# A four-layer attention kernel: its plan counts TensorE's semaphore records, and its order tables are replaced

## The chip, the cores and the metric

The kernel runs on one core of a Trainium2 chip. A core has a matrix engine (TensorE, PE in the profile; its weight loads are the rows PEld), a vector engine (VectorE, DVE), an activation engine (ScalarE, ACT), a general engine (GpSimd, POOL) and a queue engine that here only issues DMAs (SyncE, SP). Each engine works through its own instructions in order and waits on semaphores for the others. The metric is the device time of one execution in microseconds (us). Less is better.

## The reference

A stream `x` of 2048 tokens by 512 goes through four layers, A, B, A, B, each with a layer norm ahead of it and added back to the stream. Both kinds of layer have 32 heads of 16. In an A layer a token attends to 8 tokens at distances 0, 2, ..., 14 behind it; in a B layer to the 256 tokens up to itself.

```
x = A_x
x = x + A(layernorm(x), A_wqkv, A_wo)      # idx = pos - 2*arange(8), mask idx >= 0
x = x + B(layernorm(x), B_wqkv, B_wo)      # mask 0 <= q - k < 256
x = x + A(layernorm(x), A_wqkv, A_wo)
x = x + B(layernorm(x), B_wqkv, B_wo)
# in each: qkv = x @ wqkv; softmax(q k^T / 4 over the kept keys) v; concatenate heads; @ wo
```

## The kernel before

**Tiling.** The stream is cut into 8 chunks of 256 tokens. Chunk `c` of layers 0 and 1 is written by the scopes A0..A7 and B0..B7, that of layers 2 and 3 by A8..A15 and B8..B15; the scopes S, pA, pB hold constants and weights, W holds 122 TensorE tasks that compute nothing that is used (L1761). Large products are made in float16 halves: each projection part multiplies a high and a low half (L1032 to L1034 and L1052 to L1055). A layer A makes scores with small matmuls of 32 rows (L1191, 64 in one task), brings them into bands through DRAM, and mixes values with L1300 (64 in one task). A layer B stacks q and k through DRAM (puts of `re` at L1342, then `stack`), makes scores twice, once for the row maximum (L1418, reduced by VectorE at L1433) and once transposed (L1569, exponentials on ScalarE at L1579 and L1591), masks the triangles on GpSimd (L1608) or VectorE (L1602), and multiplies by the values (L1624).

**The plan.** Nothing of this is issued where it is written. Each step is a `Task` with an engine, a time, the values that it reads and writes, and buffers. `Plan.order` runs a small model of the core over all 7702 tasks and issues them in the order in which the model starts them. Within one engine the order is not the model's choice: each task has a place, a number from the table `ORDER` (one list for each scope, one number for each task), and each engine's queue is sorted by it (line 563). A negative number stands for the task's other engine: a mask on VectorE in place of GpSimd, a put on ScalarE's queue in place of SP's, and so on (line 524). So the table holds the whole order of each of the five engines and the choices between two engines, and it was found by a search that is not in the file. The model's times decide how the five queues are interleaved in the program and which PSUM bank and which buffer a task gets.

**What the model knows of instructions.** It counts TensorE's instructions as `n`, from 3, and `t.rec` for each task: 6 by default (three matmuls and three weight loads), 64 for a task of L1624, 128 for one of L1191, 129 for one of L1300. By that count it places three events in each packet of 256 instructions, and makes the task wait that reaches the third too early (lines 643 to 650; `SUPPLY` is 5.0):

```
for x in range(n + 1, n + t.rec + 1):
    if x % 256 == 152:
        mark = now + wait + us * (x - n) / t.rec
    elif x % 256 == 168:
        asked, told = told, max(mark, now, told + SUPPLY if told else 0.0)
    elif x % 256 == 193 and x > 256:
        wait = max(wait, asked + SUPPLY - now - us * (x - n) / t.rec)
n += t.rec
```

[...]

Of the kernel before, what the change touches and what calls it, by code (L numbers as in the profile page):

```python
# [19 lines left out]
S = 2048  # L20
# [5 lines left out]
W = 8  # L26
# [652 lines left out]
def kernel(  # L679
# [1084 lines left out]
    for l in (0, 2):  # L1764
        for c in range(NCH):
            n = (l // 2) * NCH + c
            plan.begin(f"A{n}")
            layer_a(l, c)
            plan.begin(f"B{n}")
            layer_b(l + 1, c)  # L1770
# [30 lines left out]
```

## Time and profile before

| | us |
|---|---|
| median of 3 runs | 1445.88 |
| lowest and highest run | 1444.29, 1458.36 |
| the profiled execution | 1450.96 |
| its span, from the first to the last instruction | 1449.2 |
| TensorE busy | 1319.0 (91%) |
| VectorE busy | 863.3 (60%) |
| ScalarE busy | 824.9 (57%) |
| GpSimd busy | 380.6 (26%) |

The mean granted TensorE clock is 0.967 of full speed. A row of the groups names the line, the engine, the operation, the tiles, the count, then the busy time, the mean of one in ns, and the idle time of that engine just before, with what ended it. A row of the waits names who waited, for whom, the sum in us, how many times, and the longest. A row of the busy times by stretches has the stretch, its length, for each engine the busy time and (x) the number of its instructions that lie in or reach into the stretch, then the granted clock, the DMA engines' busy share, and GB/s.

### The profile page before, as it was taken

The numbers are of one execution on the slowest core, as the hardware profiler recorded it, in microseconds if no ns is written. First come the engines' busy times: TensorE is split into PE (matmuls) and PEld (weight loads), VectorE is DVE, ScalarE is ACT, GpSimd is POOL, SyncE is SP. The second block draws the span as 40 slices with busy tenths as digits, with TensorE's granted clock in tenths as the row PEclk, the third lists the DMA queues.
The fourth block names the chain that finished last, engine by engine and source line by source line (L and its number), as shares of the span: only waits on it lengthen the run. The fifth ranks groups of instructions, "written<-read, shape, count | busy, mean of one in ns | idle before, by whom it ended". The sixth has DMA issues, their size and how long they took to land.

```text
span 1449.2 us, 62327 instructions
## 1 busy us (share of the span) xinstructions
PE 1319.0 (91%) x27206; PEld 844.3 (58%) x27206; DVE 863.3 (60%) x1945; ACT 824.9 (57%) x1304; POOL 380.6 (26%) x800
## 2 busy tenths in 40 slices
PE   8999999998998989889899898888989899988988
PEld 7766456574565746547465554645656465564645
DVE  6546664746657474465755536465573755728485
ACT  7654557464665736547474554737657365653554
POOL 5411122222432232112250121423132222331231
PEclk9999999999999999999999998999999999999999
DMA  9865445636364462554527464363544626445241
GB/s 297 206 179 156 111 113 140 159 97 172 99 169 113 137 164 58 160 126 137 130 76 180 122 167 119 93 169 92 170 122 137 166 75 155 105 139 134 71 113 55
DMA packets 203659, 195.08 MB, mean 135 GB/s; under 512 B 92893, under 2 KB 147933, under 8 KB 203385
## 3 DMA queue, kind: packets, MB, share of 16 engines
q1 hardware_dynamic: 177264, 172.63, 43.9%
q10 hardware_dynamic: 26120, 18.46, 5.1%
q8 instruction: 213, 3.49, 1.1%
q14 instruction: 62, 0.50, 0.1%
HBM read 94.11 MB, written 79.36 MB: 120 GB/s over the span
## 4 chain that ended last, share of the span: by engine, by line
PE 59%; DMA 10%; ACT 7%; DVE 6%; issue 6%; SPq 4%; ACTq 2%; POOL 0%; DVEq 0%; POOLq 0%
PE banks L1624 7%; PE banks L1032 7%; PE banks L1033 6%; PE banks L1034 6%; PE banks L1054 6%; PE banks L1052 5%; PE banks L1055 5%; PE banks L1418 5%; PE banks L1569 5%; PE banks L1300 3%; DVE m L1433 2%; PE banks L1191 2%; ACT p L1579 2%; DMA ptt<-ptd 1%; SPq L1342 1%
## 5 line engine op out<-in xcount | busy, mean ns | idle before, releaser
L1433 DVE TENSOR_REDUCE m<-banks 128x2 f32<-128x512 f32 x448 | 302.4, 688 | 9.0
L1579 ACT ACTIVATE p<-banks,sclB 128x896 f32<-128x896 f32 x224 | 221.1, 1008 | 87.9 <-PE banks L1569 68.2
L1437 DVE COPY_PREDICATED banks<-trm,banks 128x128 f32<-128x128 int16 x448 | 124.5, 291 | 158.1 <-PE banks L1418 131.2
L1608 POOL TENSOR_SCALAR_AFFINE_SELECT p<-p 64x256 f32<-64x256 f32 x272 | 106.7, 414 | 353.5 <-ACT p L1579 318.3
L1418 PE MATMUL banks<-stk_k,stk_q 48*64 48x320 f16 (+4 forms) x2560 | 139.6, 273 | 27.5 <-DVE m L1433 7.7
L1569 PE MATMUL banks<-stk_q,stk_k 64*64 64x256 f16 (+3 forms) x3584 | 121.4, 242 | 29.6 <-DVE m L1433 5.4
L1608 POOL TENSOR_SCALAR_AFFINE_SELECT ps<-ps 64x256 f32<-64x256 f32 x264 | 104.0, 416 | 163.3 <-ACT ps L1591 158.8
L1624 PE MATMUL banks<-p,v 64*32 64x192 f32 (+1 forms) x3584 | 119.5, 364 | 17.8 <-issue 15.0
L1418 PEld LDWEIGHTS <-stk_q 48*64 48x64 f16 x2560 | 64.1, 107 | 118.9 <-issue 103.2
L1591 ACT ACTIVATE ps<-banks,sclB 128x768 f32<-128x768 f32 x112 | 100.3, 901 | 44.0 <-PE banks L1569 32.0
L1569 PEld LDWEIGHTS <-stk_k 64*64 64x64 f16 x3584 | 71.6, 109 | 90.0 <-issue 73.5
L1200 ACT COPY s<-banks 128x624 f32<-128x624 f32 x64 | 74.7, 1260 | 44.2 <-PE banks L1191 33.0
L1638 DVE TENSOR_TENSOR os<-os,banks 128x256 f32<-128x256 f32 x112 | 46.3, 417 | 82.2 <-ACT os L1641 78.0
L1624 PEld LDWEIGHTS banks<-p,v 64*32 64x32 f32 x3584 | 63.7, 108 | 48.0 <-issue 26.2
L1641 ACT COPY os<-banks 128x256 f32<-128x256 f32 x112 | 41.4, 372 | 86.9 <-PE banks L1624 67.6
L1332 DVE SCALAR_TENSOR_TENSOR el<-banks,eh 128x512 f16<-128x512 f32 x64 | 42.6, 687 | 80.7 <-ACT eh L1329 69.2
L1624 PE MATMUL banks<-ps,v 64*32 64x64 f32 (+1 forms) x3584 | 70.0, 250 | 10.5 <-issue 10.4
L1624 PEld LDWEIGHTS banks<-ps,v 64*32 64x32 f32 x3584 | 63.7, 107 | 19.0 <-issue 16.8
L1032 PE MATMUL banks<-xh,wA1h 128*128 128x256 f16 x256 | 72.2, 282 | 1.5 <-ACT v L1367 1.5
L1032 PE MATMUL banks<-xh,wA0h 128*128 128x256 f16 x256 | 71.9, 281 | 0.9 <-issue 0.6
L1034 PE MATMUL banks<-xh,wA0l 128*128 128x256 f16 x256 | 71.3, 278 | 0.8 <-issue 0.8
L1033 PE MATMUL banks<-xl,wA1h 128*128 128x256 f16 x256 | 71.5, 279 | 0.0
(202 smaller groups left out, 3080.7 us busy)
## 6 DMA issues: line engine op xcount, KB each, us to landing
sd<-s SPq DMA_DIRECT2D x100, 156.0 KB
ptt<-ptd SPq DMA_DIRECT2D x128, 96.0 KB
stk_k<-re SPq DMA_DIRECT2D x128, 96.0 KB
stk_q<-re SPq DMA_DIRECT2D x128, 96.0 KB
re<-eh SPq DMA_DIRECT2D x82, 128.0 KB
vs<-vd SPq DMA_DIRECT2D x64, 156.0 KB
vd<-ve SPq DMA_DIRECT2D x32, 256.0 KB
xm<-y SPq DMA_DIRECT2D x32, 256.0 KB
```

What stands on the lines that cost most here:

```text
L1032: nc.tensor.matmul(ps[mp].t[:, i], wh, xh, start=k == 0, stop=False)
L1033: nc.tensor.matmul(ps[mp].t[:, i], wh, xl, start=False, stop=False)
L1034: nc.tensor.matmul(ps[mp].t[:, i], wl, xh, start=False, stop=k == 3)
L1054: nc.tensor.matmul(ps.t, xh.t[:, k, tk], wh, start=k == 0, stop=False)
L1418: nc.tensor.matmul(o, lhs, k, start=True, stop=True, tile_position=(64 * par, 64 * h))
L1433: nc.vector.tensor_reduce(out=m.t[:, :, u, qb], in_=ps.t[:, :, 0 : 2 * P], op=ALU.max, axis=AX.X)
L1437: nc.vector.copy_predicated(t[:, :, 0:64], trm[:, 0].bitcast(I16).unsqueeze(1).broadcast_to([P, 2, 64]), t[:, :, C : C + 64])
L1569: nc.tensor.matmul(ps.t[64 * h : 64 * h + 64, par, at + x0 : at + x0 + q1 - q0], stk[hf, kt][r, col, k0 : k0 + 64], stk[hf, 0][r, col, q0: ...
L1579: nc.scalar.activation(big.t[:, 2 * i : 2 * i + 2], ps.t[:, :, 0:448], AF.Exp, scale=scl["B", 1])
L1591: nc.scalar.activation(small.t.rearrange("p (i m) x -> p m i x", i=2), ps.t[:, :, 0:384].rearrange("p m (i x) -> p m i x", i=2), AF.Exp, s ...
L1608: E.affine_select(out=v, in_=v, pattern=[[0, 4], [a, 64]], compare_op=op, fill=0.0, base=0, channel_multiplier=-a)
L1624: nc.tensor.matmul(acc.t[32 * mm : 32 * mm + 32, h, q0:q1], vv[r, 17 * (H * blk + hd) : 17 * (H * blk + hd) + 32], x.t[r, mm, x0 : x0 + q1 ...
```

## The change

Three things change. A string `RECORDS` of 181 pairs `task:count` is added, and ahead of the ordering its counts are added to the tasks' `rec`; they come to 148 in sum, with numbers from -1 to 3. All 36 lists of `ORDER` are replaced by others of the same lengths. Nothing else is edited: tasks, their times, the model's constants, buffers and matmuls stay.

```diff
 ORDER = {
-    "S": [1, 16, 2, 4, 9, 0, 8, 10, 11, 15, 13],
-    "pA": [2, 4, 3, -1, 23, 1, 10, 5, -3, 4, 4, 7, 5, 9, 37, 7, 9, 16, 10, 17, 11, 8, -9, 12, -14, 10, -15, 11, -13,
-        68, 15, 29, 18, -17, 17, 19, -23, -22, -21, -21],
...
+    "S": [1, 19, 3, 0, 7, 8, 14, 2, 17, 14, 12],
+    "pA": [3, -1, 2, 4, 23, 1, 8, 4, -3, 3, 4, 7, 5, 10, 36, 7, 11, 14, 9, -9, 10, 10, -14, 6, 12, 7, 13, 11, -13, 64,
+        14, -16, 18, -17, 19, 30, 29, 20, 31, -19],
...
 }
+RECORDS = "15:1 40:1 67:1 151:1 275:1 316:-1 317:2 322:1 323:-1 470:1 473:1 492:2 526:2 538:1 550:1 572:1 643:1 675:1 715:1 716:-1 721:-1 722:1 762:1 843:2 892:1 905:1 955:1 986:1 1039:1 1051:1 1190:-1 1191:1 1196:-1 1197:3 1367:1 1473:1 1514:1 1585:1 1665:2 1666:-1 1671:2 1672:-1 1830:1 1911:1 1936:1 1952:2 2140:1 2141:-1 2146:-1 2147:2 2183:1 2187:1 2305:1 2411:2 2423:1 2535:1 2615:-1 2616:1 2621:-1 2622:2 2662:1 2758:1 2780:1 2792:1 2808:1 2833:1 2861:1 2886:1 2939:1 3018:1 3090:2 3091:-1 3096:2 3097:-1 3320:1 3414:1 3426:1 3564:1 3565:-1 3570:2 3571:-1 3729:2 3741:1 3754:1 3782:1 3794:1 3835:1 3847:1 3959:1 4040:-1 4041:2 4046:-1 4047:2 4087:1 4194:1 4204:2 4228:1 4262:1 4296:1 4379:1 4439:3 4440:-1 4445:3 4446:-1 4486:1 4576:1 4604:1 4616:1 4626:1 4657:1 4722:1 4729:1 4775:1 4842:1 4914:1 4915:-1 4920:-1 4921:2 4961:1 5079:1 5091:1 5185:1 5250:1 5337:1 5389:1 5390:-1 5395:2 5396:-1 5436:1 5520:1 5554:1 5619:1 5623:1 5691:1 5713:1 5864:2 5865:-1 5870:2 5871:-1 5907:1 6041:1 6082:1 6147:1 6287:1 6299:1 6339:1 6340:-1 6345:2 6346:-1 6382:1 6516:1 6523:1 6569:1 6579:1 6610:1 6622:1 6635:1 6663:1 6675:1 6754:1 6814:1 6815:-1 6820:-1 6821:2 6861:1 6991:1 7044:1 7150:1 7288:2 7289:-1 7294:2 7295:-1 7453:1 7470:1 7490:1 7518:1 7535:1 7561:1 7583:1 7632:1 7665:1"
 IDLE = 122
...
             plan.begin(f"B{n}")
             layer_b(l + 1, c)
+    for x in RECORDS.split():
+        plan.tasks[int(x.split(":")[0])].rec += int(x.split(":")[1])
     both = {"DVE": nc.vector, "POOL": nc.gpsimd, "ACT": nc.scalar, "SP": nc.sync}
     for t in plan.order():
         t.fn(both[t.eng]) if t.alt else t.fn()
```

787 rows, old and new, of the table ORDER are left out of this document.

## The prediction

> **What bounds the kernel now.** I read the page first, then TensorE's own waits, then the busy time by sixths of the span, then the stretches between waits.
>
> ```profile
> PE 1319.0 (91%) x27206; PEld 844.3 (58%) x27206; DVE 863.3 (60%) x1945; ACT 824.9 (57%) x1304; POOL 380.6 (26%) x800
> ...
> q8 instruction: 213, 3.49, 1.1%
> ...
> PE 59%; DMA 10%; ACT 7%; DVE 6%; issue 6%; SPq 4%; ACTq 2%; POOL 0%; DVEq 0%; POOLq 0%
> ```
>
> TensorE is busy 1319.0 of 1449.2 us, VectorE and ScalarE under 900, and PE holds 59% of the chain that ended last. So 130.2 us of the span are TensorE idle. The 213 packets of queue q8 are TensorE's instructions: 3.49 MB by 213 is 16 KB each, and 2 x 27206 recorded instructions by 213 is 255. Next, what ended TensorE's idle time. "issue" means that no instruction of the program ended it.
>
> ```profile
> PE banks L1624 <- issue: 25.5, 13, 3.6
> ...
> PE banks L1418 <- DMA stk_q<-re: 5.9, 8, 1.5
> ...
> PE banks L1569 <- issue: 5.3, 3, 3.5
> ...
> PE banks L1300 <- issue: 4.0, 4, 1.1
> PE banks L1055 <- issue: 3.8, 3, 2.4
> ...
> PE banks L1191 <- issue: 3.0, 1, 3.0
> ...
> PE banks L1034 <- issue: 1.9, 2, 1.0
> PE banks L1052 <- issue: 1.7, 1, 1.7
> ...
> PE banks L1054 <- issue: 1.4, 1, 1.4
> PE banks L1032 <- issue: 1.4, 2, 0.7
> PE banks L1418 <- issue: 1.3, 1, 1.3
> ```
>
> The ten "issue" rows hold 25.5+5.3+4.0+3.8+3.0+1.9+1.7+1.4+1.4+1.3 = 49.3 us in 31 waits; the other waits, each small, the 80.9 left of the 130.2. The largest of the 31 sits between two matmuls of one task:
>
> ```profile
> 543.15 0.99 PE L1624 MATMUL banks<-p,v 64*32 64x256 f32 x31
> ...
> 547.74 0.48 PE L1624 MATMUL banks<-p,v 64*32 64x192 f32 x1 [3.60 <-issue]
> ```
>
> That no input is missed there suggests missing instructions. The first and the last of the 31, the records between waits, and the semaphore instructions on TensorE's sequencer settle it:
>
> ```profile
> 33.38 0.46 PE L1191 MATMUL banks<-k,qm 32*64 32x39 f32 x11 [3.01 <-issue]
> ```
>
> ```profile
> 1348.79 0.21 PE L1300 MATMUL banks<-ptt,vs 39*32 39x64 f32 x1 [0.98 <-issue]
> ```
>
> ```profile
> 33.38:98.90 65.52, 63.41 (x1147) 46.73 (x1147) 37.35 (x52) 42.38 (x67) 24.38 (x25) 0.96 0.81 201
> 992.20:1163.88 171.68, 156.59 (x3571) 102.60 (x3571) 105.22 (x218) 101.08 (x159) 43.97 (x98) 1.00 0.49 136
> 1336.91:1348.78 11.87, 10.20 (x254) 4.94 (x255) 1.50 (x4) 5.90 (x7) 3.48 (x7) 0.62 0.21 64
> ```
>
> ```profile
> L1300 PEldq EVENT_SEMAPHORE  x88: 51/51/1619, 67.5 to 1345.1; - x88
> L1624 PEldq EVENT_SEMAPHORE  x58: 51/51/172, 190.9 to 1428.2; - x58
> ```
>
> From the instruction after one wait to that after another there are 1147+1147 = 2294, 3571+3571 = 7142 and 254+255 = 509 recorded instructions. With the 10, 26 and 3 semaphore instructions that the trace has in them that is 2304, 7168 and 512: 9, 28 and 2 times 256. Counted so from the start of the kernel, every one of the 31 waits stands at number 191 of its 256. They are waits for a packet of instructions.
>
> **What the plan of before counts.** It counts 54476 records, which is 2 x 27206 and one for each of the 64 `mix` tasks (rec 129). The trace has 88 semaphore instructions at L1300 and 58 at L1624, 212 over all lines; 212 - 64 = 148, and the numbers in RECORDS add up to 148. Laid along the old queue they come to 42 by 410 us, 87 by 849 and 148 at the end. So the old order was found with the packet edges put 0 to 148 records, more than half a packet, away from where they are. If that is what the waits come from, the early part must be better:
>
> ```profile
> 0.00:241.50 241.50, 225.97 (x3856) 157.83 (x3856) 142.50 (x347) 148.68 (x245) 71.85 (x133) 0.98 0.62 170
> 241.50:483.00 241.50, 223.69 (x5031) 145.95 (x5024) 154.13 (x323) 144.47 (x231) 66.09 (x148) 0.99 0.51 135
> 483.00:724.60 241.60, 215.15 (x4551) 133.22 (x4549) 141.56 (x297) 132.48 (x206) 55.17 (x121) 0.95 0.50 134
> 724.60:966.10 241.50, 218.46 (x4268) 133.85 (x4265) 126.52 (x344) 134.39 (x213) 64.34 (x126) 0.94 0.48 130
> 966.10:1207.70 241.60, 220.89 (x4953) 144.23 (x4953) 144.41 (x302) 142.52 (x224) 60.97 (x129) 0.99 0.48 130
> 1207.70:1449.20 241.50, 214.87 (x4564) 129.24 (x4561) 154.20 (x336) 122.39 (x189) 62.19 (x144) 0.95 0.41 108
> ```
>
> TensorE's idle time is 15.5 and 17.8 us in the first two sixths, and 26.5, 23.0, 20.7 and 26.6 in the others, though the first holds the start; the granted clock is 0.98 and 0.99, then 0.95, 0.94, 0.99, 0.95.
>
> **Part 1, the packets.** I took the start of each TensorE instruction in the trace and closed the 31 waits. Then I asked at each packet edge whether record 191 comes less than 4.5 us after record 160 of the packet before. 160 and 4.5 were chosen to give the trace's sum: at the true edges this finds 42 waits, 48 us, 28 of the trace's 31 among them. At the edges in which the old plan believed it finds 10, 3.0 us. Other pairs that give 47 to 50 at the true edges give 4 to 20 at the believed ones. The old order thus does avoid the waits, in the wrong places. Then I laid out the queue of the new table, each kind of task with its mean start to start in the trace (a `mix` task 0.82, a wide `value` 0.81, a third of a projection part by its three matmuls 0.365). The old queue so laid gives 55 us at the true edges and 7 at the believed; the new one, with RECORDS, 7 (18 waits), and 13 by the worst pair. With the count 20 records off it gives 8 to 23, 30 off 11 to 32, 60 off up to 58. I take 12 us, near the worst pair: chip times vary, so a tuned margin is not all kept. 49.3 - 12 = **37.3 us less**; bounds 49.3 - 7 = 42 and, with the count 30 off, 49.3 - 30 = 19.
>
> [...]
>
> **Part 2, the clock.** After ten of the 31 waits the granted clock is half; three of these stretches, the sum over the ten (each at 0.50), and the wait ahead of the third:
>
> ```profile
> 547.20:553.90 6.70, 6.16 (x23) 2.68 (x22) 2.34 (x5) 1.53 (x4) 0.28 (x1) 0.50 0.13 44
> 1335.70:1345.80 10.10, 8.20 (x126) 3.53 (x127) 2.67 (x6) 4.54 (x6) 2.42 (x2) 0.50 0.34 95
> 731.50:734.80 3.30, 3.30 (x36) 1.39 (x35) 1.92 (x4) 0.63 (x2) 0.00 (x0) 0.50 0.23 53
> sum 49.93, PE 44.49 PEld 19.61 DVE 22.36 ACT 18.23 POOL 9.58; mean PE 4.45 PEld 1.96 DVE 2.24 ACT 1.82 POOL 0.96
> ```
>
> ```profile
> 729.57 0.34 PE L1624 MATMUL banks<-ps,v 64*32 64x64 f32 x15 [1.48 <-issue]
> ```
>
> TensorE is busy 44.49 us in them, and half of that, 22.2 us, is what the slow clock cost. If 12 of the 49.3 us of waits stay, 22.2 x 37.3 / 49.3 = **16.8 us** go. Bounds: 0, if other waits pull the clock down in the same places, and 22.
>
> [...]
>
> **Part 3, everything else in the tables.** No instruction of TensorE is added or taken out. Of its 3472 tasks 1712 would have to be lifted out to make the two queues agree, so waits on other engines are dealt anew. VectorE's queue goes from 1720 to 1713 tasks, ScalarE's from 1299 to 1304, GpSimd's from 360 to 372, SP's from 851 to 841. The changes of engine nearly cancel: 54 masks go from VectorE to GpSimd and 47 back, 44 puts of `re` from SP to ScalarE and 34 back.
>
> ```profile
> L1608 POOL TENSOR_SCALAR_AFFINE_SELECT p<-p 64x256 f32<-64x256 f32 x272 | 106.7, 414 | 353.5 <-ACT p L1579 318.3 <-PE banks L1052 18.5 <-ACT mt L1456 9.0
> L1602 DVE COPY_PREDICATED_SCALAR ps<-trm,nul 128x512 f32 x46 | 36.2, 790 | 29.9 <-ACT ps L1591 29.6
> ```
>
> ```profile
> L1342 ACTq DMA_DIRECT2D re<-eh x46: 525/594/1982, 104.1 to 1373.9; - x46
> ```
>
> A mask is four GpSimd instructions of 414 ns or one VectorE instruction of 790: 7 more on GpSimd add 12 us there, and take 5.5 from VectorE. Ten more puts are 10 x 0.594 = 6 us of ScalarE's queue, taken from SP's; behind each put stands ScalarE's next activation, and TensorE waits for that only if it is late for a matmul. All three engines idle 40% of the time or more (page, first row); without that cover the 12 and the 6 would come on top. I take 0 for the other waits: 80.9 us dealt anew. Bounds: they fall by 23 if the last four sixths become like the first two (TensorE idle without packets is 33.3 - 14.1 = 19.3 there, 14.1 being the ten packet waits before 483 us, and 61.6 in the others; 61.6 - 2 x 19.3), and rise by 15, twenty waits of the 0.74 us of the L1418 row above. That the first two have less of both kinds speaks against the packet waits merely giving way to others.
>
> **Sum.** 37.3 + 16.8 + 0 = 54.1 us. The profiled execution took 1450.96 us, 1.8 beyond its span: 1450.96 - 54.1 = **1397 us**. The median before, 1445.88, is 5 us lower than that execution, and the runs shown reach from 1444.29 to 1458.36, so I leave 1397 as it is. A check by another way: if the last four sixths had the idle time of the first two, 96.8 - 2 x 33.3 = 30 us go; their half-clock time, 2 x (1 - clock) x 241.5, is 82 against 2 x 14.5, and half of that surplus by the busy share 0.89 is 24. That is 54 also, and bounds the gain without any rule for the edges.
>
> **The rivals.**
> (a) The count is stale. Line by line RECORDS fits the program of before (58 more at L1624, 24 more at L1300 than the 64 already counted), and the new order may need its semaphores elsewhere. 30 off on the whole leaves 29 us of waits and 29/49.3 of the clock's 22.2, so a gain of 20 + 9 = 29: 1422. It decides from about 60 off on: then nothing is gained. Against it: 148 semaphores would have to become under 90 or over 200 with the same work. Chance 0.14.
> (b) The change doesn't do what it says: packets come late because data fills the DMA engines, not because edges fall into dense code, and the waits stay: 1449. For it: the first wait, at 30 us, falls in the busiest DMA time. Against it: the DMA share is 0.41 in the last sixth, which has five of the 31 waits and 8.5 us, and 0.62 in the first, which has four and 6.0 us. [...] Chance 0.07.
> (c) Slower: the puts at L1342 now on ScalarE's queue stand behind one activation of L1579 and two issues.
>
> ```profile
> L1579 ACT ACTIVATE p<-banks,sclB 128x896 f32<-128x896 f32 x224 | 221.1, 1008 | 87.9 <-PE banks L1569 68.2 <-DMA rc<-os 13.6 <-DMA re<-eh 2.5
> ```
>
> Each of the 32 stacks (16 B layers, q and k) then lands 1.008 + 2 x 0.594 = 2.2 us late, and scores at L1418 wait: 32 x 2.2 = 70, so 1397 + 70 = 1467. It decides from 2.1 us a stack on, where it eats 54 + 14.5. Against it: L1418 waits for `stk_q<-re` only 8 times for 5.9 us now, with 63 puts on ScalarE already. Chance 0.05.
> (d) Better: the other waits fall by the 23 us too, since a plan true in its packets is true in its times: 1374. Chance 0.1.
> The forecast keeps 0.64.
>
> **Numbers.** One per cent is 14.5 us, about what a measurement of this kernel can tell from no change: faster means under 1431. That holds the forecast, (d), and nearly all of (a): 0.64 + 0.1 + 0.13 = 0.87. Same: (b) and the rest of (a), 0.08. Slower: (c), 0.05. The range from 1376 to 1428 holds the forecast with its bounds (a gain from 19 + 5, with a third of the clock's term, to 42 + 22 + 11, with half of the 23), most of (a), and half of (d); it leaves out (b), (c), and the rest of these.
>
> **What would show it.** Right: "issue" rows of TensorE's waits adding up to 5 to 20 us, no wait over 2 us among them, at number 191 of a packet still; half-clock time, 2 x (1 - 0.967) x 1449 = 96 us now, near 60; the sixths alike. Step 1 is wrong if the waits stay over 30 us; step 2 if the clock stays near 0.967 without them; part 3 if the other waits exceed 100 us. A count of semaphores far from 148 + 64 would be (a).

## The result and the profile after

The changed kernel takes 1411.24 us, the median of 4 runs (1408.02 to 1414.15), against 1449.11 (1444.29 to 1458.36, also 4) for the kernel before. The ratio is 0.973, with a 95% interval of 0.967 to 0.979. A run over 1.5% above the fastest of its kernel counts as slow and is left out of the medians and ratios here and below; that is so for three of the ten runs of one kernel, the one shifted by 60. The changed kernel's profiled execution took 1414.15 us with a span of 1412.4, so 36.8 us less than the one before. In the changed file a line of the kernel's code has a number two higher than before (L1626 is the old L1624).

The page of the changed kernel, its first row and its instruction queue:

```profile
PE 1308.5 (93%) x27206; PEld 841.8 (60%) x27206; DVE 852.2 (60%) x1932; ACT 825.8 (58%) x1303; POOL 405.9 (29%) x839
...
q8 instruction: 213, 3.49, 1.1%
```

TensorE's idle time is 1412.4 - 1308.5 = 103.9 us, 26.3 less; its busy time is 10.5 us less with the same 27206 matmuls. These two are the gain: 26.3 + 10.5 = 36.8. The packets of instructions are the same 213. TensorE's own waits in the changed kernel (who waited for whom, us in total, times, the longest): the longest rows and every row of "issue".

```profile
PE banks L1571 <- DMA stk_q<-md: 8.4, 6, 4.2
PE banks L1420 <- DVE m L1435: 7.0, 18, 0.9
PE banks L1571 <- DVE m L1435: 5.4, 12, 0.7
PE banks L1034 <- ACT v L1369: 4.7, 4, 2.9
PE banks L1056 <- DVE m L1435: 4.2, 2, 2.2
...
PE banks L1420 <- DMA stk_q<-re: 3.5, 5, 2.1
...
PE banks L1511 <- issue: 2.5, 1, 2.5
PE banks L1626 <- issue: 1.9, 3, 1.1
...
PE banks L1763 <- issue: 1.3, 1, 1.3
...
PE banks L1056 <- issue: 0.7, 1, 0.7
...
PE banks L1302 <- issue: 0.6, 1, 0.6
```

"issue" led this list before, with 49.3 us in 31 waits; now it is 2.5+1.9+1.3+0.7+0.6 = 7.0 us in 7. The other waits went the other way, from 80.9 to 103.9 - 7.0 = 96.9 us, and no single one of them stands out. (Of the 96.9 the rows hold 86.0; the rest lies in gaps too short for a row and behind the last matmul.) The semaphore instructions of TensorE's sequencer, and TensorE by sixths of the span (the second number is the time that it was busy, the third from the end the granted clock):

```profile
L1302 PEldq EVENT_SEMAPHORE  x89: 51/51/1161, 67.9 to 1307.7; - x89
```

```profile
L1626 PEldq EVENT_SEMAPHORE  x63: 51/51/263, 188.1 to 1388.2; - x63
```

```profile
0.00:235.40 235.40, 220.43 (x3706) 154.91 (x3707) 135.92 (x340) 147.23 (x244) 75.50 (x128) 0.99 0.62 170
235.40:470.80 235.40, 217.14 (x4874) 135.59 (x4872) 146.16 (x307) 133.56 (x213) 56.24 (x127) 0.96 0.54 140
470.80:706.20 235.40, 218.25 (x4693) 140.92 (x4692) 137.75 (x293) 140.33 (x217) 74.54 (x166) 0.96 0.49 134
706.20:941.60 235.40, 220.22 (x4418) 136.68 (x4417) 136.15 (x362) 140.02 (x223) 62.78 (x119) 0.96 0.50 139
941.60:1177.00 235.40, 224.25 (x4967) 145.01 (x4966) 142.34 (x300) 141.57 (x222) 74.76 (x158) 0.99 0.52 139
1177.00:1412.40 235.40, 208.23 (x4556) 128.65 (x4556) 153.92 (x333) 123.11 (x189) 62.05 (x142) 0.98 0.40 107
```

The first two sixths have 33.2 us of idle TensorE, as before (33.3); the last four have 70.7 in place of 96.8. By its idle time, then, TensorE gained where the count had been off by 42 records and more. The packet waits by themselves say less than that. All rows of "issue" up to 470.8 us, and all behind it:

```profile
PE banks L1763 <- issue: 1.3, 1, 1.3
...
PE banks L1626 <- issue: 1.3, 2, 1.1
...
PE banks L1056 <- issue: 0.7, 1, 0.7
...
PE banks L1302 <- issue: 0.6, 1, 0.6
```

```profile
PE banks L1511 <- issue: 2.5, 1, 2.5
...
PE banks L1626 <- issue: 0.6, 1, 0.6
```

They fell in both parts, from 14.1 to 3.9 us in the first two sixths and from 35.2 to 3.1 in the last four. The other waits rose from 19.3 to 29.3 in the first two, as much as the packet waits fell there, and from 61.6 to 67.6 in the last four.

### The profile page after: what moved, and what is told of

Its sections match the earlier page's. It is cut to its first block, busy times and chain, and to the rows that moved or that the text cites. A ratio compares the mean times of both kernels' runs of the same rounds, so it can differ in the third digit from the quotient of the medians.

```text
span 1412.4 us, 62375 instructions
## 1 busy us (share of the span) xinstructions
PE 1308.5 (93%) x27206; PEld 841.8 (60%) x27206; DVE 852.2 (60%) x1932; ACT 825.8 (58%) x1303; POOL 405.9 (29%) x839
## 4 chain that ended last, share of the span: by engine, by line
PE 59%; DMA 11%; DVE 10%; ACT 7%; SPq 4%; issue 4%; POOL 2%; ACTq 1%; DVEq 0%; POOLq 0%
PE banks L1034 7%; PE banks L1626 7%; PE banks L1035 6%; PE banks L1036 6%; PE banks L1056 5%; PE banks L1054 5%; PE banks L1571 4%; PE banks L1057 4%; PE banks L1420 4%; DVE m L1435 3%; PE banks L1193 3%; PE banks L1302 3%; ACT p L1581 2%; DMA stk_q<-re 2%; DVE banks L1439 1%
## 5 line engine op out<-in xcount | busy, mean ns | idle before, releaser
L1610 POOL TENSOR_SCALAR_AFFINE_SELECT ps<-ps 64x256 f32<-64x256 f32 x300 | 118.2, 416 | 252.3 <-ACT ps L1593 231.2
L1610 POOL TENSOR_SCALAR_AFFINE_SELECT p<-p 64x256 f32<-64x256 f32 x264 | 103.1, 412 | 214.7 <-ACT p L1581 206.6
L1420 PE MATMUL banks<-stk_k,stk_q 48*64 48x320 f16 (+4 forms) x2560 | 139.5, 274 | 24.5 <-DVE m L1435 7.0
L1420 PEld LDWEIGHTS <-stk_q 48*64 48x64 f16 x2560 | 65.7, 107 | 107.5 <-issue 94.8
L1626 PE MATMUL banks<-p,v 64*32 64x192 f32 (+1 forms) x3584 | 112.6, 355 | 6.1 <-ACT p L1581 1.8
L1626 PEld LDWEIGHTS banks<-p,v 64*32 64x32 f32 x3584 | 62.9, 106 | 37.6 <-issue 13.0
L1036 PE MATMUL banks<-xh,wA1l 128*128 128x256 f16 x256 | 71.5, 279 | 0.0
L1035 PE MATMUL banks<-xl,wA0h 128*128 128x256 f16 x256 | 71.3, 279 | 0.0
```

What stands on the lines that cost most here:

```text
L1035: nc.tensor.matmul(ps[mp].t[:, i], wh, xl, start=False, stop=False)
L1036: nc.tensor.matmul(ps[mp].t[:, i], wl, xh, start=False, stop=k == 3)
L1420: nc.tensor.matmul(o, lhs, k, start=True, stop=True, tile_position=(64 * par, 64 * h))
L1610: E.affine_select(out=v, in_=v, pattern=[[0, 4], [a, 64]], compare_op=op, fill=0.0, base=0, channel_multiplier=-a)
L1626: nc.tensor.matmul(acc.t[32 * mm : 32 * mm + 32, h, q0:q1], vv[r, 17 * (H * blk + hd) : 17 * (H * blk + hd) + 32], x.t[r, mm, x0 : x0 + q1 ...
```

## The experiments

All seven renumber TensorE's instructions and leave the order of every engine, every bank, buffer and engine choice as the plan made them. They do it in the idle tasks at L1761, which multiply a constant into a bank that nothing reads: an idle task makes its 768 columns in six matmuls, or in two, in place of three, which is 6 records more or 2 fewer (in the shift by 256, in twelve shorter ones, 18 more).

```diff
     plan.begin("W")
+    early = sorted(range(IDLE), key=lambda i: ORDER["W"][i])
...
             v = idf.bitcast(F16)
+            if i in early[:10]:
+                for _ in range(6):
+                    nc.tensor.matmul(junk.t[0:128, 0:128], v[:, 0:128], v[:, 0:128], start=True, stop=True)
+                return
             for _ in range(3):
                 nc.tensor.matmul(junk.t[:, 0 : 2 * P], v[:, 0:P], v, start=True, stop=True)
```

**The changed kernel, 60 records later.**

> The changed kernel with 60 records more on TensorE ahead of everything: ten of the idle tasks at the start make their 768 columns in six matmuls and not in three. No order, bank, buffer or engine differs; only the edges of the packets of instructions fall 60 records earlier in the work. Theory 1 (the gain is that packet edges fall where the order has time for them): the changed kernel's trace, with its packet waits closed and the edges moved by 60, gives 52 to 58 us of packet waits in place of 7, and the clock goes down after some of them as before the change, 11 to 15 us: about 1411 + 45 + 13 = 1469 us. If the other waits (97 us now, 81 before the change) are what the packet waits had covered, they fall by some 16 again: 1453. Theory 2 (the new orders are better by themselves, or packets come late because of other DMA traffic): no change, 1405 to 1417.

Measured: 1452.7 us (7 runs), ratio to the kernel before 0.998, 0.994 to 1.002. All of the gain is gone, with 30 more matmuls among 27206. Rows of "issue" among TensorE's waits:

```profile
PE banks L1420 <- issue: 8.4, 5, 3.9
PE banks L1302 <- issue: 7.2, 4, 2.2
...
PE banks L1034 <- issue: 5.8, 3, 3.7
```

The rows of "issue" add up to 38.9 us in 27 waits, fewer than the 52 to 58 worked out. The other waits fall to 83.7. The time is the 1453 that was worked out with the other waits falling, but not by the terms of that sum: in the profiled execution, of 1446.4 us, the packet waits rose by 31.9 and not by 45, the other waits fell by 13.2 and not by 16, and TensorE's busy time rose by 13.6. Theory 2 would have had 1405 to 1417.

**The changed kernel, 128 and 256 records later.** The same edit, with 21 tasks and one matmul more, and with 14 tasks of twelve matmuls and two more.

> As the shift by 60, with 128 records, half a packet. Theory 1: 58 to 79 us of packet waits by the same working, about 1411 + 57 + 16 = 1484 us, 16 less if the other waits fall again. Theory 2: 1405 to 1417.

> As the shift by 60, with 256 records, one whole packet: the edges fall where they fell. It costs what 128 short matmuls at the start cost, which TensorE has time for there. Theory 1: 4 to 12 us of packet waits, 1408 to 1418 us, although it adds more instructions than the other two shifts. If it is the added instructions or the start that cost, it is slower than the shift by 128.

Measured: 1439.38 us by 128 (ratio 0.989, 0.983 to 0.994) and 1413.86 by 256 (0.973, 0.969 to 0.977). Waits of TensorE in the kernel shifted by 128, then all of "issue" in the one shifted by 256:

```profile
PE banks L1302 <- issue: 18.6, 13, 3.5
PE banks L1193 <- issue: 7.8, 7, 2.7
PE banks L1420 <- DVE m L1435: 5.8, 16, 0.8
```

```profile
PE banks L1771 <- issue: 2.7, 1, 2.7
...
PE banks L1626 <- issue: 2.3, 4, 1.3
...
PE banks L1302 <- issue: 1.5, 4, 0.7
PE banks L1056 <- issue: 1.4, 1, 1.4
...
PE banks L1571 <- issue: 0.2, 1, 0.2
```

A whole packet more is the changed kernel again (8.1 us of packet waits, in the changed kernel 7.0), half a packet is not (38.0). The shift by a whole packet has most instructions added and the shortest time of the three shifts, so neither the number of added instructions nor the start costs the time, and no traffic of other DMAs explains it: what counts is where in the work the edges fall. (Its added matmuls are shorter, 64 columns in place of 128.) The shift by 128 costs less than worked out (28 us and not 57 + 16) and, unlike the working, less than the shift by 60.

**The kernel before, 60 records earlier.**

```diff
...
+            if i in early[:30]:
+                x = v[:, 0:192].unsqueeze(1).broadcast_to([P, 2, 192])
+                for _ in range(2):
+                    nc.tensor.matmul(junk.t[:, 0:384].rearrange("p (a b) -> p a b", a=2), v[:, 0:P], x, start=True, stop=True)
+                return
```

> The kernel before with 60 records fewer on TensorE at the start: 30 idle tasks make their 768 columns in two matmuls and not in three. Its plan and every order stay. The plan's count is then 60 records ahead at the start and 88 behind at the end, in place of 0 and 148. Theory 1: 18 to 31 us of packet waits in place of 49 by the trace of before, 6 to 10 us less lost to the clock: 1449 - 25 - 8 = 1416 us; 1424 if part of what goes turns into other waits. Theory 2 (the gain is in the new orders): 1445 to 1453.

Measured: 1416.98 us, ratio 0.973, 0.967 to 0.979, which is the changed kernel's ratio to the last digit given. Old tables, old plan, no RECORDS. All of its "issue" rows:

```profile
PE banks L1624 <- issue: 3.4, 2, 2.3
PE banks L1569 <- issue: 3.3, 4, 1.0
PE banks L1767 <- issue: 3.3, 1, 3.3
...
PE banks L1418 <- issue: 3.1, 3, 1.5
...
PE banks L1300 <- issue: 0.7, 1, 0.7
...
PE banks L1054 <- issue: 0.6, 1, 0.6
...
PE banks L1191 <- issue: 0.4, 1, 0.4
```

14.8 us in 13 waits, under the 18 to 31 worked out, and 92.2 us of other waits, 11 more than before. Theory 2 falls here for good: no new order is needed for the gain.

**The kernel before, 52 records fewer, most of them taken out between 70 and 440 us.** The same edit in 26 idle tasks, two at the start and 24 between 85 and 439 us.

> The kernel before with 52 records fewer, 48 of them taken from idle tasks between 70 and 440 us instead of at the start, so that its count is right early and 50 ahead to 96 behind later. Plan and orders are the old ones. By the trace of before, closed and renumbered: 13 to 25 us of packet waits. Theory 1a (what the packets lose is all that matters, about 0.9 us of time for each us of packet waits, from 49 us at 1450 and 7 us at 1411): 1417 to 1428. If the new orders are worth something beside the packets, this stays 10 us or more above the changed kernel at the same packet waits; if not, it lies on one line with it, as the old order with 60 records fewer did (15 us, 1417).

Measured: 1416.75 us, ratio 0.977, 0.975 to 0.979, with 13.3 us of "issue" and 91.2 of other waits. It lies with the changed kernel and the last one, just under the 1417 to 1428 expected. All rows of "issue" up to 470.1 us, a third of its span:

```profile
PE banks L1569 <- issue: 1.3, 2, 0.7
...
PE banks L1418 <- issue: 1.2, 1, 1.2
...
PE banks L1191 <- issue: 0.3, 1, 0.3
```

That is 2.8 us where before has 14.1. The plan does not count 45 of the semaphore instructions in this third, and the idle tasks here lose about as many records, so its count is never more than some 12 records off, against up to 45 before (both counted in the traces; later it goes from some 6 ahead to 96 behind, so the 50 ahead that was expected is not so). That fits waits that come from a lagging count. It does not prove it, for the order moved by 60 records, with its count 60 to some 15 ahead there, has no more than 5.7 us in its first third.

**The changed kernel, 20 records later.** Three tasks of six matmuls and one matmul more.

> The changed kernel with 20 records more at the start. By its trace renumbered: 17 to 20 us of packet waits in place of 7. By 0.9 us for each: 1420 to 1424 us. If the order keeps its distance from the edges by more than 20 records, nothing: 1408 to 1414. The other waits, 97 us in the changed kernel, should fall to about 90 if packet waits cover others one for three.

Measured: 1416.06 us, ratio 0.976, 0.971 to 0.980; 20.0 us of "issue", as worked out, and 88.7 of other waits. The time lies between the two expectations, as do its other waits (90 were expected), and its runs (1407 to 1421) hold the unchanged 1411, so the time alone decides nothing here; the profile does.

**The kernel before, 60 records later.**

> The kernel before with 60 records more at the start, the mirror of the one with 60 fewer: its count is then 60 to 208 behind. By the trace of before renumbered: 64 to 71 us of packet waits in place of 49; by the two shifts of the new kernel, which gave 39 where 52 to 79 were worked out, some two thirds of that, 45 to 50. Time 1446 to 1462 us: no faster than before. If taking records away or adding them at the start is itself what helped the kernel with 60 fewer, this one differs from before by as much the other way, 30 us slower, or is faster too.

Measured: 1453.2 us (10 runs), ratio 1.001, 0.999 to 1.003, as expected. "issue" is 52.9 us, in 34 waits, between the two figures worked out; the longest rows of TensorE's waits:

```profile
PE banks L1624 <- issue: 24.5, 13, 4.3
PE banks L1300 <- issue: 14.8, 8, 4.0
PE banks L1191 <- issue: 7.2, 7, 2.1
PE banks L1418 <- DVE m L1433: 6.4, 18, 0.7
```

Adding to the start of the old order isn't taking away with the sign turned round: it was bad already with its count 0 to 148 records behind, and is as bad with 60 to 208.

**The nine profiles together.** "Packets" is the sum of TensorE's "issue" rows, "others" the rest of its idle time, all in us of the profiled execution:

| kernel | packets | others | PE busy | span | median of its runs |
|---|---|---|---|---|---|
| before | 49.3 | 80.9 | 1319.0 | 1449.2 | 1449 to 1453 |
| before, +60 | 52.9 | 73.8 | 1326.0 | 1452.7 | 1453.2 |
| before, -60 | 14.8 | 92.2 | 1314.4 | 1421.4 | 1417.0 |
| before, -52 | 13.3 | 91.2 | 1305.8 | 1410.3 | 1416.8 |
| after | 7.0 | 96.9 | 1308.5 | 1412.4 | 1411.2 |
| after, +20 | 20.0 | 88.7 | 1310.1 | 1418.8 | 1416.1 |
| after, +60 | 38.9 | 83.7 | 1322.1 | 1444.7 | 1452.7 |
| after, +128 | 38.0 | 78.9 | 1318.7 | 1435.6 | 1439.4 |
| after, +256 | 8.1 | 93.9 | 1310.8 | 1412.8 | 1413.9 |

Counted as in the trace of before, 182 of the 187 waits of "issue" in these nine profiles stand at the same place of their 256, to within one record, wherever the edges had been moved to in the work. A straight line through the nine has others = 97.9 - 0.41 x packets (correlation -0.96), busy = 1305.9 + 0.34 x packets (0.90), span = 1403.7 + 0.93 x packets (0.98), the last with no point more than 6 us off. As the span is the sum of the three columns, 0.93 is no finding of its own: it is 1 - 0.41 + 0.34. Old and new orders lie on both sides of it (old: -0.2, 0, +4.0, -5.7; new: +2.2, -3.4, +5.0, -3.3, +1.6), so at equal packet waits neither table is seen to be better, as far as points that lie up to 6 us off can tell.

## Why the prediction was right, and where it was off

**The time and its direction.** 1411 lies in the range of 1376 to 1428, 14 us above the 1397 predicted. The gain is 36.8 us where 54.1 were worked out: the packets gave 5.0 more, the clock 6.3 less, and the other waits took 16.0.

**Part 1 was right in mechanism and nearly in size.** 12 us were to stay of the 49.3 and 37.3 to go; 7.0 stayed and 42.3 went, which is the value that the laid-out queue gave (7) before I rounded it up. Six of the seven waits in the changed kernel, 6.4 of the 7.0 us, stand at number 191 of their 256 again. One sign was missed: no wait was to be over 2 us, and one, at L1511, is 2.5. A second row of evidence is in the trace of before: ahead of each of its 21 "issue" waits of over 1 us, a transfer of the instruction queue q8 landed 1.2 to 1.6 us before TensorE went on. By number few packets show a wait: 6 of the 213 in the changed kernel, 31 before. By time they are not little: the 31 were 49.3 us, and the same instructions as in the changed kernel, moved by 60, have 38.9 in 27 waits.

**Part 2 was sized too large.** 16.8 us were to go and TensorE's busy time fell by 10.5. I gave the whole half-clock time after ten packet waits to them. The clock went from 0.967 to 0.974:

```profile
core 0: 1449.2 us, clock 0.967
```

```profile
core 0: 1412.4 us, clock 0.974
```

so the half-clock time, 2 x (1 - clock) x span, went from 96 to 73 us, not to near 60 (the traces of before and after show the clock at 1.00 or at 0.50, and the stretches at 0.50, 21 before and 14 after, last 96.5 and 73.3 us); half of these 23 us, by TensorE's busy share of 0.9, is 10 by estimate, near the 10.5 measured. Only one stretch of half clock follows a packet wait now, the 2.5 us at L1511:

```profile
806.60:810.00 3.40, 3.40 (x10) 1.20 (x9) 1.03 (x5) 2.23 (x5) 2.64 (x3) 0.50 0.22 82
```

Ten of the 13 others begin during a wait of 1.4 to 3.6 us on another engine or a DMA, or within 2.7 us after its end, and the waits of that kind grew, from 80.9 to 96.9 us.

**Part 3 is the step that failed.** "I take 0 for the other waits", with a bound of +15, and they rose by 16.0, to 96.9, short of the 100 that was to be the sign. I had argued that the first two sixths, with fewer waits of both kinds, speak against one giving way to the other. The five kernels of the new order, which differ only in the numbering and the dummy matmuls that make it, show the opposite: 38 to 39 us of packet waits go with 79 to 84 of others, 7 to 8 with 94 to 97. That fits this account, which no run shows step by step: while TensorE waits for instructions the other engines go on, and their results are there when TensorE comes for them; take the wait away and TensorE arrives early. By the line 0.41 of each us comes back: 0.41 x 42.3 = 17, measured 16.0. That is a mean over the kernel. In the first two sixths all of what the packets lost there came back (10.2 us less, 10.0 more), in the last four about a fifth (32.1 less, 6.0 more). So the first two, on which the argument rested, are just where the packet waits gave way to others. With the two measured sizes the sum is 42.3 + 10.5 - 16.0 = 36.8. The check by sixths had nearly the idle time (26 of the 30 us, all in the last four), but by luck in part: it took the first two as free of what was to go, and they had 14.1 us of packet waits, which went and came back as others. The sixths did not become alike either: the last has 27.2 us of idle time, before 26.6. The check was too large in the clock: by the clocks shown, the half-clock time of the last four sixths went from 82 to 52, and that of the first two rose from 14.5 to 23.5.

**The rivals.** (a) did not come: the changed program has 89 semaphore instructions at L1302 and 63 at L1626, 210 over all lines where the program of before had 212, so RECORDS is 2 off at the end. The shift by 20 shows what 20 records off would cost (20 us of packet waits), the shift by 60 that it decides where (a) said, from about 60 on. (b) is refuted by the shift of a whole packet against that of half a one. (c): L1420 waited for `stk_q<-re` 3.5 us in 5 waits, before 5.9 in 8, so the moved puts cost nothing that can be seen. (d) was wrong in its sign: the other waits rose.

**What was not foreseen at all** is that the tables need not have changed. The order of before, with 30 matmuls fewer among the idle ones at the start, gives 0.973 as well. That the new tables lie well at the edges because they were found with a true count fits the shifts, all of which but the whole packet are worse, but the search was not repeated without it. Neither part of the change was run alone (RECORDS with the old tables, the new tables without RECORDS). That the new tables are better otherwise is not shown.

**Open.** Moving the edges of the changed kernel by 60 and by 128 gave 39 and 38 us of packet waits where its trace, closed and renumbered, gave 52 to 58 and 58 to 79. That waits elsewhere leave more room at the edges than the closed trace has would fit, but was not tried by itself. Nor is it settled why the shift by 60 is 13 us slower than that by 128 at the same packet waits. Their profiled executions are 9 us apart: that of the shift by 60 has 3 us of busy time more, at the lower clock (0.965 against 0.972), 5 us of other waits, and 1 of packets. The rest is that both profiled executions are faster than the medians of their runs, 1446.4 by 6 us and 1437.29 by 2.

## What to carry to other kernels

When TensorE's longest waits end in nothing that the program did, count its records between them, semaphore instructions too: here the distances were multiples of 256 (2304, 7168 and 512), the waits were for packets of instructions, and a few dummy matmuls more or fewer at the start, moving the edges, both proved it and could cure it (60 records fewer took the old order from 1453 to 1417 us and its packet waits from 49.3 to 14.8, 60 more left it at 1453 and 52.9). A count that a plan keeps over tens of thousands of instructions has to be checked against the trace late in the run, where its small errors have added up (here to 148 of 54624). And price a removed stall with what it sets off: here, on the mean, 0.41 of each us came back as other waits, 0.34 more was won in TensorE's busy time, which was longest at the lowest clock (1326.0 us at 0.962) and shortest at the highest (1305.8 at 0.976), and the net was 0.93.

## What the runs showed of the hardware that I had not expected

A program's time can change by 3% through its numbering alone: 30 more matmuls of 128 columns at the start took the changed kernel from 1411 to 1453 us, and 128 shorter ones left it at 1414. The sensitivity is steep: 20 records, a thirteenth of a packet, took the packet waits from 7.0 to 20.0 us, and 60 to 38.9.
